# Weight conversion with half the VectorE operations, its pieces listed among the first two groups' chunks

## The chip, the cores and the metric

The kernel runs on one core of a Trainium2 chip. The metric is device microseconds of one execution, as the median of three runs; less is better. The profile is one further execution, recorded by the hardware profiler. PE is TensorE, DVE is VectorE, ACT is ScalarE, POOL is GpSimd and SP is SyncE, whose queue issues nearly all transfers.

## The reference

A gated linear attention (state decayed by a complex gate at every step) feeds a two-layer block with the activation h * cos(h). The two weight matrices arrive as float64, everything else as float32.

```python
mag = sqrt(a_re**2 + a_im**2);  scale = minimum(mag, 0.999) / (mag + 1e-6)
for t in range(768):                                  # B, H, D = 4, 8, 48
    S = (a * scale)[t] * S + outer(k[t], v[t])        # complex gate, real k and v
    y[t] = q[t] @ S.real
x = y.reshape(3072, 384)
h = x @ w_in                                          # w_in [384, 2048], float64
out = (h * cos(h)) @ w_out                            # w_out [2048, 384], float64
```

## The kernel before

The 3072 tokens are 24 chunks of 128 steps; two chunks form a group, so there are 12 groups. The program is a software pipeline over groups. In iteration `it` it emits the gate mathematics of group `it` (`g_log`, `g_prod`, `g_angle`, then `g_phase`, `g_trig`, `g_stack` as `gates`), the attention of group `it - 1` chunk by chunk (`chunks`: transposes `tp`, scores `sc`, state update `sp`, output `yp`, transpose `xp` into `xT`), the first matrix product `mm1` of group `it - 2` (`hp`, then the cosine) and the second, `mm2`, of group `it - 3` (`op`, then the store). `weave` interleaves such lists by a fractional position for each item. A scheduler of the framework then fixes each engine's order; every engine takes its instructions strictly in that order, and so does the SP queue with its transfers.

The gate mathematics of a group is one long chain. ACT takes squares, logarithm and exponentials (L633 to L641), POOL subtracts (`m`, L646), PE forms running sums over the steps (`lgs`, L662), ACT exponentiates them (L663, L664), DVE combines them and closes the angle (`sq`, L688), PE sums the angle (`phs`, L697 and L700), DVE rounds it (`ph`, L702, L704), ACT takes sine and cosine (L712, L713), and DVE builds `ks` and `qs` (L722), which the transposes of the chunk read. DVE masks the scores (`atm`, L746). In `mm1` ACT scales (`turn`, L802), DVE reduces (`cs`, L803, L805), ACT takes the sine, and DVE multiplies by `hp` (`gate`, L807). Lines that go through the helper `special` are recorded as L619, its table loads as L618.

The weights are converted from float64 on the chip. `weight_parts` cuts them into 12 pieces of `w_in` (128 x 512) and 16 of `w_out` (128 x 384); `from_double` loads a piece as 64-bit words into `raw` (two buffers), shifts and joins the words' halves `lo` and `hi` on DVE (L588, L590, L592), takes the rounding bit (L594), adds it on POOL (L596), and clears values too small for float32 (L598, L600). All 28 pieces are woven into iteration 0, beside the gates of group 0:

```python
if it == 0:
    weave((gates(0), 0.0, 1.0), (weights, 0.2, 1.0))
    continue
```

`mm1` of a group needs all of `w_in`, `mm2` all of `w_out`. `gate` has 12 buffers of which a group fills 8; `turn` and `cs` have two each. At the end of the program the flag from `least` decides whether a general path runs; with these inputs it doesn't.

Of the kernel before, what the change touches and what calls it, by code (L numbers as in the profile page):

```python
# [485 lines left out]
def fast_path(ctx, tc, q, k, v, a_re, a_im, moe_w_in, moe_w_out, out, least):  # L486
# [88 lines left out]
    def from_double(dst, src):  # L575

        n = dst.shape[1]
        raw = stage.tile([C, n], I64, tag="raw", name="raw")
        nc.sync.dma_start(out=raw, in_=src)
        words = raw.bitcast(U32).rearrange("p (x two) -> p x two", two=2)
        lo, hi = words[:, :, 0], words[:, :, 1]
        t = stage.tile([C, n], U32, tag="t", name="t")
        bits = dst.bitcast(U32)
        nc.vector.tensor_scalar(out=bits, in0=hi, scalar1=3, scalar2=0x3FFFFFF8,  # L588
                                op0=ALU.logical_shift_left, op1=ALU.bitwise_and)
        nc.vector.scalar_tensor_tensor(out=bits, in0=hi, scalar=0xC0000000, in1=bits,  # L590
                                       op0=ALU.bitwise_and, op1=ALU.bitwise_or)
        nc.vector.scalar_tensor_tensor(out=bits, in0=lo, scalar=29, in1=bits,  # L592
                                       op0=ALU.logical_shift_right, op1=ALU.bitwise_or)
        nc.vector.tensor_scalar(out=t, in0=lo, scalar1=28, scalar2=1,  # L594
                                op0=ALU.logical_shift_right, op1=ALU.bitwise_and)
        nc.gpsimd.tensor_tensor(out=bits, in0=bits, in1=t, op=ALU.add)  # L596
        e = stage.tile([C, n], U32, tag="t", name="t")
        nc.vector.tensor_scalar(out=e, in0=hi, scalar1=20, scalar2=0x7FF,  # L598
                                op0=ALU.logical_shift_right, op1=ALU.bitwise_and)
        nc.vector.scalar_tensor_tensor(out=dst, in0=e, scalar=897.0, in1=dst,  # L600
                                       op0=ALU.is_ge, op1=ALU.mult)
# [135 lines left out]

    def f_scores(n, hh):
# [4 lines left out]
        for h in range(HH):  # L743
            nc.tensor.matmul(ps[:, h], lhsT=y["kT"][:, hh * HH + h], rhs=y["qT"][:, hh * HH + h],  # L744
                             start=True, stop=True)
# [17 lines left out]
    def f_state(n):  # L763
# [4 lines left out]
        for h in range(H):  # L768
            nc.tensor.matmul(ps[:, h], lhsT=X[g]["ks"][:, i * H + h].rearrange("p a d -> p (a d)"),  # L769
                             rhs=X[g]["v"][:, i, h], start=True, stop=True)  # L770
# [20 lines left out]
    def mm1(g, jp):  # L791
# [8 lines left out]
        cs = msb.tile([C, 2, G * C], F32, tag="cs", name="cs")  # L800
        gate = msb.tile([C, 2, G * C], F32, tag="gate", name="gate", bufs=12)
        nc.scalar.activation(out=turn, in_=ps, func=AF.Identity, scale=INV_TWO_PI, bias=quarter_b)  # L802
# [7 lines left out]
    def mm2(g, i):  # L810
# [5 lines left out]
        nc.scalar.copy(out=ot, in_=ps)  # L816
# [33 lines left out]
    weights = weight_parts()  # L850
    for it in range(NG + 3):
# [9 lines left out]
        if it == 0:  # L861
            weave((gates(0), 0.0, 1.0), (weights, 0.2, 1.0))
            continue
        if 0 <= o < NG:
            for i in range(G):
                mm2(o, i)
        weave((gates(g) if g < NG else (), 0.0, 0.5),
              (chunks(c) if 0 <= c < NG else (), 0.0, 1.0),
              ([lambda jp=jp: mm1(m, jp) for jp in range(NJ // 2)] if 0 <= m < NG else (),
# [4 lines left out]
def kernel(ctx, tc, q, k, v, a_re, a_im, moe_w_in, moe_w_out, out):  # L874
# [7 lines left out]
    fast_path(tc, q, k, v, a_re, a_im, moe_w_in, moe_w_out, out, least)  # L882
    low = keep.tile([D2, 1], F32, name="low")
    nc.vector.tensor_reduce(out=low, in_=least, axis=AX.X, op=ALU.min)
    scratch = ctx.enter_context(tc.tile_pool(name="scratch", bufs=1,
                                             space=bass.MemoryType.DRAM))
    line_d = scratch.tile([D2], F32, name="line_d")
    nc.sync.dma_start(out=line_d, in_=low.rearrange("p o -> (p o)"))
    line = keep.tile([1, D2], F32, name="line")
# [39 lines left out]
```

## Time and profile before

| | |
|---|---|
| median of three runs | 931.01 us (930.38 to 933.06) |
| the profiled execution | 938.23 us, its span 936.4 us |
| mean granted TensorE clock | 0.943 |
| PE busy | 797.1 us (85%) |
| DVE busy | 497.1 us (53%) |
| ACT busy | 378.6 us (40%) |
| POOL busy | 171.3 us (18%) |

Busy shares are means over the whole span, and the start differs from the rest. How to read the rows below: the slices are fortieths of the span, with a digit for tenths of busy time; the stage table gives busy time per engine in chosen stretches; a timeline row begins with its start and its length, and ends, in brackets, with the engine's idle time before it and what ended that.

### The profile page before, as it was taken

The page shows a single profiled execution, that of the slowest core. Times are in us where ns is not written, and L with a number is a line of the kernel's source. Part 1 is how long each engine was busy: PE and PEld are TensorE (multiplying, and loading weights), DVE is VectorE, ACT ScalarE, POOL GpSimd, SP SyncE. Part 2 cuts the span into 40 slices and gives each one's busy share as a digit, 9 for nine tenths or more (in the row PEclk, how much of TensorE's full clock was granted, in tenths as well). Part 3 has the DMA queues.
Part 4 walks back from the last instruction along what each step waited for, and adds up shares of the span by engine and source line. Part 5 has one row for each costly group of instructions (what it writes and reads, how often), then busy time and mean ns, then how long its engine had stood idle before and what let it go on. Part 6 is the DMA issues. An engine that isn't in the chain of part 4 may idle for free.

```text
span 936.4 us, 10169 instructions
## 1 busy us (share of the span) xinstructions
PE 797.1 (85%) x3920; PEld 621.0 (66%) x3920; DVE 497.1 (53%) x761; ACT 378.6 (40%) x588; POOL 171.3 (18%) x96
## 2 busy tenths in 40 slices
PE   1101446899999999999999999999999989999997
PEld 0000245685885977967968858858769668778684
DVE  3999985844544736636545446346456445123160
ACT  5222123535454554454364454354544623123140
POOL 2343333403103022112120031031030211000000
PEclk9999966899899999989899999898999998998999
DMA  8523631303004004004023040040040100000000
GB/s 174 141 90 112 146 108 34 69 18 63 23 18 85 1 18 85 1 17 85 1 43 60 18 83 3 18 85 1 18 84 1 26 10 1 9 9 1 9 8 21
DMA packets 151876, 42.03 MB, mean 45 GB/s; under 512 B 144638, under 2 KB 148222, under 8 KB 151818
## 3 DMA queue, kind: packets, MB, share of 16 engines
q1 hardware_dynamic: 151218, 40.98, 19.8%
q8 instruction: 33, 0.54, 0.3%
q10 hardware_dynamic: 600, 0.30, 0.1%
q14 instruction: 25, 0.20, 0.1%
HBM read 36.51 MB, written 4.76 MB: 44 GB/s over the span
## 4 chain that ended last, share of the span: by engine, by line
PE 70%; ACT 6%; DVE 2%; POOL 2%; DMA 1%; issue 1%; ACTq 0%; SPq 0%; POOLq 0%; DVEq 0%
PE hp L796 28%; PE op L813 17%; PE yp L755 4%; PE sc L744 4%; PE yp L758 4%; PE tp L734 4%; PE sp L769 3%; POOL m L646 2%; ACT rs L619 2%; PE lgs L662 1%; ACT L618 1%; PE phs L697 1%; PE phs L700 1%; PE xp L788 1%; ACT m L619 1%; ACT mag L619 1%
## 5 line engine op out<-in xcount | busy, mean ns | idle before, releaser
L796 PE MATMUL hp<-xT,w_in 128*128 128x256 f32 x1152 | 294.0, 409 | 4.1 <-DVE gate L807 3.5
L796 PEld LDWEIGHTS hp<-xT,w_in 128*128 128x128 f32 x1152 | 231.0, 207 | 39.7 <-DVE gate L807 3.9
L813 PE MATMUL op<-w_out,gate 128*128 128x384 f32 x768 | 251.1, 486 | 0.0
L813 PEld LDWEIGHTS op<-w_out,gate 128*128 128x128 f32 x768 | 145.9, 190 | 99.2
L803 DVE TENSOR_SCALAR cs<-turn 128x512 f32<-128x512 f32 x96 | 42.4, 443 | 172.9 <-ACT turn L802 172.9
L802 ACT ACTIVATE turn<-hp,quarter_b 128x512 f32<-128x512 f32 x96 | 65.7, 685 | 124.6 <-PE hp L796 122.7
L807 DVE TENSOR_TENSOR gate<-hp,cs 128x512 f32<-128x512 f32 x96 | 66.2, 690 | 82.2 <-ACT cs L619 81.4
L776 POOL TENSOR_TENSOR state<-state,end 96x384 f32<-96x384 f32 x16 | 31.2, 1949 | 342.2 <-DVE state L774 179.1
L755 PE MATMUL yp<-v,atm 128*128 128x48 f32 x384 | 75.3, 292 | 19.3 <-DVE atm L746 19.3
L619 ACT ACTIVATE cs<-cs 128x512 f32<-128x512 f32 x96 | 60.5, 630 | 69.0 <-DVE cs L805 69.0
L662 PE MATMUL lgs<-m,sums 128*128 128x384 f32 x48 | 21.3, 572 | 64.6 <-POOL m L646 49.3
L755 PEld LDWEIGHTS yp<-v,atm 128*128 128x128 f32 x384 | 62.0, 209 | 20.4 <-DVE atm L746 20.2
L758 PE MATMUL yp<-state,qT 96*128 96x48 f32 x320 | 67.7, 296 | 0.0
L805 DVE TENSOR_TENSOR cs<-turn,cs 128x512 f32<-128x512 f32 x96 | 65.9, 687 | 2.1
L662 PEld LDWEIGHTS lgs<-m,sums 128*128 128x128 f32 x48 | 9.2, 211 | 75.2 <-POOL m L646 71.3
L646 POOL TENSOR_TENSOR m<-m,rs 128x768 f32<-128x768 f32 x12 | 22.0, 1835 | 197.6 <-ACT rs L619 196.7
L697 PE MATMUL phs<-sq,sums 128*128 128x384 f32 x48 | 22.4, 557 | 38.8 <-DVE sq L688 38.8
L758 PEld LDWEIGHTS yp<-state,qT 96*128 96x128 f32 x320 | 54.2, 212 | 0.0
L761 ACT COPY x<-yp 128x384 f32<-128x384 f32 x24 | 11.5, 478 | 104.6 <-PE yp L758 94.0
L633 ACT ACTIVATE m<-re 128x768 f32<-128x768 f32 x12 | 10.1, 842 | 97.3 <-DMA re<-in_a_re_dram 97.3
L744 PE MATMUL sc<-qT,kT 96*128 96x128 f32 x384 | 48.4, 277 | 0.1
L744 PEld LDWEIGHTS sc<-qT,kT 96*128 96x128 f32 x384 | 46.9, 192 | 2.3 <-ACT qT L736 1.0
(77 smaller groups left out, 955.0 us busy)
## 6 DMA issues: line engine op xcount, KB each, us to landing
raw<-in_moe_w_in_dram SPq DMA_DIRECT2D x12, 512.0 KB
raw<-in_moe_w_out_dram SPq DMA_DIRECT2D x16, 384.0 KB
re<-in_a_re_dram SPq DMA_DIRECT2D x24, 192.0 KB
im<-in_a_im_dram SPq DMA_DIRECT2D x24, 192.0 KB
k<-in_k_dram SPq DMA_DIRECT2D x24, 192.0 KB
q<-in_q_dram SPq DMA_DIRECT2D x24, 192.0 KB
v<-in_v_dram SPq DMA_DIRECT2D x24, 192.0 KB
out_dram<-ot SPq DMA_DIRECT2D x24, 192.0 KB
```

Of the source, the lines that this page charges most:

```text
L619: chain(nc.scalar.activation(func=func, **kw))
L646: nc.gpsimd.tensor_tensor(out=m2, in0=m2, in1=rs, op=ALU.subtract)
L662: nc.tensor.matmul(ps, lhsT=sums, rhs=x["lg"][:, ts(i, DM)], start=True, stop=True)
L744: nc.tensor.matmul(ps[:, h], lhsT=y["kT"][:, hh * HH + h], rhs=y["qT"][:, hh * HH + h], start=True, stop=True)
L755: nc.tensor.matmul(ps[:, h], lhsT=y["atm"][:, h], rhs=vals[:, h], start=True, stop=(state is None))
L758: nc.tensor.matmul(ps[:, h], lhsT=y["qT"][:, h], rhs=state[:, h], start=False, stop=True)
L796: nc.tensor.matmul(ps[:, ji], lhsT=w_in[:, dc, ts(jp * 2 + ji, C)], rhs=x["xT"][:, dc].rearrange("p g t -> p (g t)"), start=(dc == 0), sto ...
L802: nc.scalar.activation(out=turn, in_=ps, func=AF.Identity, scale=INV_TWO_PI, bias=quarter_b)
L803: nc.vector.tensor_scalar(out=cs, in0=turn, scalar1=ROUND, scalar2=ROUND, op0=ALU.add, op1=ALU.subtract)
L805: nc.vector.tensor_tensor(out=cs, in0=turn, in1=cs, op=ALU.subtract)
L807: nc.vector.tensor_tensor(out=gate, in0=ps, in1=cs, op=ALU.mult)
L813: nc.tensor.matmul(ps, lhsT=X[g]["gate"][j // 2][:, j % 2, ts(i, C)], rhs=w_out[:, j], start=(j == 0), stop=(j == NJ - 1))
```

## The change

Of a piece's six DVE operations three are left. DVE moves the high word into place (L592 and L594 of the new kernel), and takes the exponent (L598) into `e`, which has one buffer. ACT turns the low word into the missing bits in one operation (`low`, L596), which POOL adds (L597), and sums over each row how far exponents fall below the limit (L600); the sums go to `odd`, which is reduced once and joins the flag at the end, instead of a clearing of each value. The converted weights are twice the true ones, and the scales of `turn` and of the copy out of `mm2` undo that.

The list of pieces is cut in two: `w_in` is woven into iteration 1, among group 0's chunks, `w_out` into iteration 2, among group 1's chunks and the first `mm1`. Iteration 0 is now woven like the others. The reduced angle of `mm1` is written into the gate's own buffer, and the tile `cs` is gone.

```diff
-        t = stage.tile([C, n], U32, tag="t", name="t")
+        low = stage.tile([C, n], U32, tag="low", name="low")
+        e = stage.tile([C, n], U32, tag="e", name="e", bufs=1)
...
-        nc.vector.scalar_tensor_tensor(out=bits, in0=lo, scalar=29, in1=bits,
-                                       op0=ALU.logical_shift_right, op1=ALU.bitwise_or)
-        nc.vector.tensor_scalar(out=t, in0=lo, scalar1=28, scalar2=1,
-                                op0=ALU.logical_shift_right, op1=ALU.bitwise_and)
-        nc.gpsimd.tensor_tensor(out=bits, in0=bits, in1=t, op=ALU.add)
-        e = stage.tile([C, n], U32, tag="t", name="t")
-        nc.vector.tensor_scalar(out=e, in0=hi, scalar1=20, scalar2=0x7FF,
-                                op0=ALU.logical_shift_right, op1=ALU.bitwise_and)
-        nc.vector.scalar_tensor_tensor(out=dst, in0=e, scalar=897.0, in1=dst,
-                                       op0=ALU.is_ge, op1=ALU.mult)
+        nc.scalar.activation(out=low, in_=lo, func=AF.Identity, scale=2.0 ** -29, bias=carrier_b)
+        nc.gpsimd.tensor_tensor(out=bits, in0=bits, in1=low, op=ALU.add)
+        nc.vector.tensor_scalar(out=e, in0=hi, scalar1=1, scalar2=21,
+                                op0=ALU.logical_shift_left, op1=ALU.logical_shift_right)
+        nc.scalar.activation(out=e.bitcast(F32), in_=e, func=AF.Relu, scale=-1.0, bias=least_e_b,
+                             accum_out=odd[:, ds(next(odds), 1)])
...
-        cs = msb.tile([C, 2, G * C], F32, tag="cs", name="cs")
         gate = msb.tile([C, 2, G * C], F32, tag="gate", name="gate", bufs=12)
-        nc.scalar.activation(out=turn, in_=ps, func=AF.Identity, scale=INV_TWO_PI, bias=quarter_b)
+        cs = gate
+        nc.scalar.activation(out=turn, in_=ps, func=AF.Identity, scale=INV_TWO_PI / in_scale,
+                             bias=quarter_b)
...
-        nc.scalar.copy(out=ot, in_=ps)
+        nc.scalar.mul(out=ot, in_=ps, mul=1.0 / (in_scale * out_scale))
...
-    weights = weight_parts()
+    parts = weight_parts()
+    weights = {1: parts[:-NJ], 2: parts[-NJ:]}
...
-        if it == 0:
-            weave((gates(0), 0.0, 1.0), (weights, 0.2, 1.0))
-            continue
...
               (chunks(c) if 0 <= c < NG else (), 0.0, 1.0),
+              (weights.get(it, ()), 0.0, 1.0),
```

DVE's order at group 0's phase, before: behind the last rounding of the phase (`ph`) conversions stand between each pair of the group's own operations, here up to `ks`.

```order
L704 TENSOR_TENSOR ph<-phs,ph 128x384
L588 TENSOR_SCALAR w_in<-raw 128x512
L600 SCALAR_TENSOR_TENSOR w_in<-t,w_in 128x512
...
L710 TENSOR_SCALAR trig<-ph 128x768
...
L635 TENSOR_TENSOR m_515<-m_515,sq 128x768
...
L722 TENSOR_TENSOR ks<-Q,trig 128x1536
```

The same place on DVE in the new kernel:

```order
L711 TENSOR_TENSOR ph<-phs,ph 128x384
L642 TENSOR_TENSOR m_213<-m_213,sq 128x768
L717 TENSOR_SCALAR trig<-ph 128x768
L729 TENSOR_TENSOR ks<-Q,trig 128x1536
L729 TENSOR_TENSOR qs<-P,trig 128x1536
L592 TENSOR_SCALAR w_in<-raw 128x512
```

The conversions have moved from between `ph`, `trig` and `ks` to behind `qs`.

DVE's order in iteration 2, between the phase of group 2 and its `trig`, before:

```order
L702 TENSOR_SCALAR ph<-phs 128x384
L746 TENSOR_TENSOR atm<-sc,causal 128x512
L704 TENSOR_TENSOR ph<-phs,ph 128x384
...
L710 TENSOR_SCALAR trig<-ph 128x768
L774 SCALAR_TENSOR_TENSOR state<-sp,state 96x384
```

The same place in the new kernel, where `w_out` is converted:

```order
L709 TENSOR_SCALAR ph<-phs 128x384
L756 TENSOR_TENSOR atm<-sc,causal 128x512
L711 TENSOR_TENSOR ph<-phs,ph 128x384
L818 TENSOR_TENSOR gate<-hp,gate 128x512
L592 TENSOR_SCALAR w_out<-raw 128x384
L598 TENSOR_SCALAR e<-raw 128x384
L594 SCALAR_TENSOR_TENSOR w_out<-raw,w_out 128x384
L717 TENSOR_SCALAR trig<-ph 128x768
```

Pieces of `w_out` now stand between the operations of group 2, where there was none.

SP's queue around the second half of the weights, before (`end` is the small transfer that closes a group's `g_prod`; `im`, `k`, `re` and `q` are a group's inputs):

```order
L541 DMA q<-in_q_dram 128x8x48 x2
L583 DMA raw<-in_moe_w_out_dram 128x384 x9
L541 DMA v<-in_v_dram 128x8x48 x2
L541 DMA im<-in_a_im_dram 128x8x48 x2
L541 DMA k<-in_k_dram 128x8x48
L675 DMA end<-row 48x16x1 x2
```

The same in the new kernel:

```order
L542 DMA im<-in_a_im_dram 128x8x48 x2
L586 DMA raw<-in_moe_w_out_dram 128x384
L542 DMA k<-in_k_dram 128x8x48
L682 DMA end<-row 48x16x1 x2
L542 DMA re<-in_a_re_dram 128x8x48 x2
L586 DMA raw<-in_moe_w_out_dram 128x384 x2
L542 DMA k<-in_k_dram 128x8x48
L542 DMA q<-in_q_dram 128x8x48 x2
L586 DMA raw<-in_moe_w_out_dram 128x384 x9
```

All pieces of `w_out` from the fourth on now stand behind `end` of group 2.

## Rows read from the trace of the kernel before

**Rows 1.** Page, busy tenths in 40 equal slices of the span

```profile
PE   1101446899999999999999999999999989999997
PEclk9999966899899999989899999898999998998999
```

**Rows 2.** Busy time by stage; columns PE, PEld, DVE, ACT, POOL, clock, DMA, GB/s

```profile
28.35:73.49 45.14, 4.58 (x6) 1.68 (x7) 41.84 (x65) 10.39 (x12) 19.16 (x11) 1.00 0.44 122
73.49:105.86 32.37, 3.78 (x8) 1.96 (x8) 31.21 (x49) 5.55 (x9) 13.03 (x9) 1.00 0.46 110
105.86:156.01 50.15, 28.22 (x155) 24.23 (x155) 38.70 (x88) 11.25 (x18) 17.32 (x13) 0.71 0.36 103
156.01:173.43 17.42, 13.87 (x48) 10.65 (x49) 10.65 (x13) 11.95 (x18) 6.80 (x4) 0.79 0.16 31
173.43:209.15 35.72, 35.72 (x227) 31.61 (x227) 21.89 (x34) 15.56 (x26) 5.96 (x3) 0.89 0.25 45
209.15:232.54 23.39, 22.19 (x69) 12.78 (x68) 11.17 (x12) 12.60 (x17) 8.37 (x4) 1.00 0.25 47
232.54:936.40 703.86, 685.85 (x3407) 536.94 (x3405) 327.89 (x484) 297.87 (x473) 92.32 (x45) 0.96 0.14 29
```

**Rows 3.** Waits before 160 us: who waited for whom, total, times, longest

```profile
PE phs L697 <- DVE sq L688: 38.8, 2, 28.6
PE lgs L662 <- POOL m L646: 38.6, 1, 38.6
PE yp L755 <- DVE atm L746: 19.3, 3, 11.3
```

**Rows 4.** Timeline, one w_in piece and POOL's add: start, length, instruction

```profile
51.99 0.42 DVE L594 TENSOR_SCALAR t<-raw 128x512 uint32<-128x512 uint32 x1
52.32 0.69 DVE L592 SCALAR_TENSOR_TENSOR w_in<-raw,w_in 128x512 uint32<-128x512 uint32 x1
...
53.09 1.37 POOL L596 TENSOR_TENSOR w_in<-w_in,t 128x512 uint32<-128x512 uint32 x1 [2.35 <-DVE w_in L592]
53.26 1.49 DVE L588 TENSOR_SCALAR w_in<-raw 128x512 uint32<-128x512 uint32 x1
```

**Rows 5.** Timeline, one w_out piece, POOL's add, and a product that reads PSUM

```profile
128.06 0.55 DVE L592 SCALAR_TENSOR_TENSOR w_out<-raw,w_out 128x384 uint32<-128x384 uint32 x1
128.53 0.35 DVE L598 TENSOR_SCALAR t<-raw 128x384 uint32<-128x384 uint32 x1
128.69 1.04 POOL L596 TENSOR_TENSOR w_out<-w_out,t 128x384 uint32<-128x384 uint32 x1 [1.88 <-DVE w_out L592]
128.80 0.68 DVE L746 TENSOR_TENSOR atm<-sc,causal 128x512 f32<-128x512 f32 x1
```

**Rows 6.** Groups by line and form: count, busy us, mean ns, idle before

```profile
L807 DVE TENSOR_TENSOR gate<-hp,cs 128x512 f32<-128x512 f32 x96 | 66.2, 690 | 82.2 <-ACT cs L619 81.4
...
L619 ACT ACTIVATE cs<-cs 128x512 f32<-128x512 f32 x96 | 60.5, 630 | 69.0 <-DVE cs L805 69.0
...
L619 ACT ACTIVATE P<-lgs 128x384 f32<-128x384 f32 x24 | 11.8, 492 | 24.3 <-PE lgs L662 24.3
```

**Rows 7.** Timeline, the gate chain of group 0 and of group 3

```profile
9.21 0.93 ACT L619 ACTIVATE m<-m,tiny_b 128x768 f32<-128x768 f32 x1 [1.03 <-DVE m L635]
...
28.35 2.93 PE L697 MATMUL phs<-sq,sums 128*128 128x384 f32 x4 [10.18 <-DVE sq L688]
...
43.97 0.94 ACT L619 ACTIVATE trig<-trig,half_pi_b 128x768 f32<-128x768 f32 x1 [4.33 <-DVE trig L710]
...
213.32 0.94 ACT L619 ACTIVATE m<-m,tiny_b 128x768 f32<-128x768 f32 x1
...
226.23 2.45 DVE L688 SCALAR_TENSOR_TENSOR sq<-sq,rs 128x768 f32<-128x768 f32 x1
```

**Rows 8.** Timeline of SyncE's queue: a row merges issues of one kind

```profile
38.32 37.29 SPq L583 DMA_DIRECT2D raw<-in_moe_w_in_dram  x8
...
111.46 29.23 SPq L583 DMA_DIRECT2D raw<-in_moe_w_out_dram  x9
```

## What is predicted, and how

> **What bounds the kernel now.** I read the page's slices first. In [rows 1] TensorE (PE) stands at 1, 1, 0, 1, 4, 4, 6 tenths in its first seven slices of 23.4 us and at 8 or 9 from the eighth on: the span is a start of about 165 us in which PE mostly waits, and a long stretch in which it is full. The second view, busy time by stage [rows 2], cuts the start at the points where PE gets something new: first phase matmul of group 0 (28.35), first running log sum of group 1 (73.49), first phase matmul of group 1 (105.86), first mm1 (156.01), phase of group 2 (173.43), first mm2 (209.15), the transposes behind that mm2 (232.54). Up to 105.86 VectorE is busy for 41.84 of 45.14 and 31.21 of 32.37 us, and PE for 8.4 us in both together. From 173.43 on PE is busy for 35.72 of 35.72, and for 685.85 of the last 703.86 us. The third view, waits before 160 us [rows 3], names who ends PE's long idle times: POOL's `m`, VectorE's `sq` and `atm`, all of which stand in queues between weight conversions. So the path runs through VectorE until about 150 us and through PE afterwards. Behind 232.54 the order on PE is the same row for row in both kernels, so what can change is the time at which that point is reached, unless the full stretch itself runs at another speed.
>
> **What the change does, by cost.** A w_in piece now has three VectorE shifts at 0.42 us and three two-input operations at 0.68 to 0.69 [rows 4]: 3.3 us. It keeps two of the first and one of the second: 1.52. A w_out piece goes from 3 x 0.35 + 3 x 0.55 = 2.7 to 1.25 us [rows 5]. Over 12 and 16 pieces VectorE loses 21.4 + 23.2 = 44.6 us of work. POOL's add stays, 1.37 and 1.04 us, and it isn't free to VectorE: the shift issued at 53.26, while that add ran, took 1.49 instead of 0.42 [rows 4]. But the `atm` product, which reads PSUM, took its usual 0.68 beside an add of 1.04 [rows 5]. I therefore count POOL's adds as VectorE time except beside PSUM readers. The Trainium skill (SBUF — State Buffer, Who interferes with whom) says the same of the shared port, that the blocked engine waits for the other's whole instruction; both rows agree.
>
> ScalarE gains two operations a piece. The trace has no such form; the nearest rows are 0.63 us at 512 columns and 0.49 at 384 [rows 6], so 12 x 1.26 + 16 x 0.98 = 31 us, and up to twice that if the strided read or the accumulated sum costs extra. In the start ScalarE is busy for 10.39, 5.55, 11.25, 11.95, 15.56 and 12.60 us in 204 [rows 2]; I take the 31 as covered there. The Trainium skill speaks against this move (ScalarE: Activation LUTs, Rules for kernel authors): it wants additions and Relu on VectorE. With the fixed cost and the rate that the same skill page gives for ScalarE, the 56 operations would be an estimated 36 us, which the idle time would cover too.
>
> The other half is the move. The pieces leave the first iteration: two w_in pieces still stand ahead of the first phase (VectorE's order is filled early), the other ten come among group 0's chunks, and all of w_out comes among group 1's chunks and the first mm1. Stage by stage, what the new start should be:
>
> (1) First phase matmul: two more conversion operations and one add ahead of it, 28.35 becomes about 31.
>
> (2) Phase of group 0 to phase of group 1. From 28.35 to the end of the second sine at 43.97 + 0.94 [rows 7] there are 16.6 us, with about three pieces' VectorE work between; without them about 8.2, then the table load: the logarithm of group 1 starts near 40. From there, group 0 needed 28.35 - 9.21 = 19.1 us to its phase matmul, and group 3, with no conversions about, 226.23 + 2.45 - 213.32 = 15.4 [rows 7]. Three w_in pieces lie in this chain now, 3 x (1.52 + 1.37) = 8.7, about two thirds of it in the way. 40 + 19 + 6 = 65, against 105.86. Ends: 55 (nothing in the way) and 70 (all of it and another POOL turn).
>
> (3) To the first mm1: it took 50.15 us with twelve w_out pieces in VectorE's queue [rows 2]. PE's own work is 28.22 us at a granted clock of 0.71; VectorE's is now four w_in pieces (11.6) and the group's own operations. I take 29, so 94 against 156.01. Ends: 22 (the same PE work at full clock and two waits) and 40.
>
> (4) To the phase of group 2: 17.42 before, a chain of the same kind as in (2); the last w_in and first w_out pieces join it, mostly while PE finishes the chunk. 19, so 113. Ends 15 and 27.
>
> (5) From there to the last w_out piece. VectorE's 21.89 and POOL's 5.96 us [rows 2] get 14 pieces x (1.25 + 1.04) = 32 more: 59.9 if nothing overlaps; eight gate products at 0.69 [rows 6] and the four score products at 0.68 [rows 5], with the phase roundings some 11 us, read PSUM, of which I let half lie beside POOL: 54, so 167. Ends: 35.72, where PE alone sets the pace, and 60. PE was full here, so this stage becomes longer, not shorter: VectorE takes the bound back for one iteration.
>
> (6) From the last piece mm2 still has one matmul of its first and sixteen of its second chunk to do, half of the 23.39 us [rows 2] and the wait for the log sums and phase of group 3, which are now closer behind: 15, so 182 against 232.54.
>
> That is 50 us. PE's order lists each conversion's followers strictly, and ScalarE's in-order queue has operations that wait for a piece's transfer; I take 5 off for such waits: **45 us**. Transfers themselves: with two buffers, eight w_in pieces were issued in 37.29 us and nine w_out in 29.23 [rows 8], 4.66 and 3.25 us a piece, paced by VectorE then; 14 x 3.25 = 45.5 would fit under the 54 of (5).
>
> The remaining edits I cost at nothing: the cosine written into the gate's buffer uses one of 12 buffers, of which mm2 has released eight before mm1 needs the ninth; the scaled copy out of mm2 is the same ScalarE operation 24 times, off the path but for the last; the flag's extra reductions and row come before mm2 of group 0. If the gate's cover failed it would be PE waiting in every iteration, and the stretch behind 232.54 would show it.
>
> **Rivals.** (A) POOL and VectorE overlap better than counted, or PE reaches mm2's order first, so stage (5) is PE's 36 to 37 us: mm2 starts near 113 + 36, the join is at 149 + 23.4 = 172, a gain of 60: 871. For it: PE was full there before. Against: 32 us of added VectorE and POOL work where 8 us were free.
>
> (B) Transfers and ScalarE's in-order queue set the pace: SyncE's queue puts the w_out pieces from the fourth on behind `end` of group 2 and the loads of group 3, and each later piece needs its buffer back. With 4.66 instead of 3.25 us a piece [rows 8], 14 x 4.66 = 65 us in stage (5) and a like excess of 4 to 5 us in stage (3): the gain falls to about 30, 901. For it: the addition of waits on an engine that also copies kT and qT. Against: it never showed in the start of before, where VectorE was later than the transfers.
>
> (C) Slower. The same mechanism at full price: the steps above hold about 53 us for conversions (6, 11, 5 and 26 in stages (2) to (5), and the 5 of waits), so a start with none on its path joins at 187 - 53 = 134. If 26 pieces (all but the first two) each held ScalarE's queue for a whole unhidden 4.66 us, that is 121 us on top: the join falls at 255, 22 us late, 953. It decides from (232.54 - 134) / 26 = 3.8 us unhidden per piece. Two buffers, with the next piece's transfer in flight, speak against it.
>
> (D) The gain is given back: the full stretch runs at a granted clock of 0.96 [rows 2], between lower and full level; 45 of 686 us come back if the mean falls to 0.90. PE's order there is unchanged, and the clock fell only around the long waits in 105.86 to 209.15 (0.71, 0.79, 0.89), so nothing points to it. About 931.
>
> **How the numbers follow.** The profiled execution took 938.23 us with a span of 936.4; the median of the three runs is 931.01. The 45 us come from the profiled span, which becomes 891; on the median 931.0 - 45 = **886 us**. Chances: forecast 0.55, A 0.18, B 0.20, C 0.04, D 0.03. For the range I put the ends of (2) to (5) together as independent: shorter by 10, 7, 4 and 18 gives 22 us more gain, longer by 5, 11, 8 and 6 gives 16 less. That is 864 to 902; I take 866 to 904, so that B lies in it and A does. A measurement of this kernel can tell about 0.3% from no change (2.8 us); all but C and D is faster by far more: faster 0.94, same 0.03, slower 0.03.
>
> **What would show it.** In the profile after: no slice under 3 tenths for PE beyond the third; first phase matmul of group 1 near 65, first mm1 near 94, first mm2 between 149 and 169, the transposes behind it near 187; VectorE at 9 tenths until about 165 with POOL's adds between, and PE below full in stage (5). Of the stretch behind the join, 703 us long as before to within 5. Rival A would show PE full from 113; B waits of ScalarE or VectorE on `raw`; C the same with each piece apart; D a lower clock behind the join. I am wrong if the start's chain isn't VectorE's: if stage (2) keeps over 60 us without VectorE being busy, something that this trace hides under it (loads, POOL) sets it.

## The result, and the profile after

| | before | after |
|---|---|---|
| median of four runs each, on one chip | 932.03 us (930.38 to 935.01) | 870.79 us (868.33 to 878.84) |
| the profiled execution, its span | 938.23, 936.4 us | 878.84, 877.0 us |
| mean granted TensorE clock | 0.943 | 0.952 |

The ratio is 0.9355 with a 95% interval of 0.9285 to 0.9424: 61 us faster, where 45 were forecast. The profiled span is 59.4 us shorter. From here on medians and spreads are of all executions of a kernel, and ratios leave out those over 1.5% above its fastest.

The slices of the changed kernel, which answer to [rows 1], with VectorE's beside them:

```profile
PE   1229889899999999999999999999999989999997
...
DVE  3888889664464464464473464464473464034060
...
PEclk9998789989999999999998989999999978989999
```

PE is at 8 or 9 tenths from the fourth slice on, at 66 us, and not from the eighth. VectorE is at 8 or 9 tenths from the second to the seventh.

The stage table of the changed kernel (PE, PEld, DVE, ACT, POOL with their counts, clock, DMA, GB/s), cut at the points of [rows 2], but for the first log sum of group 1: phase of group 0, phase of group 1, first mm1, phase of group 2, first mm2, the transposes behind it:

```profile
30.50:63.94 33.44, 8.31 (x15) 3.65 (x15) 27.25 (x31) 21.53 (x33) 14.19 (x8) 1.00 0.51 129
63.94:91.43 27.49, 25.08 (x155) 21.27 (x155) 23.67 (x35) 20.34 (x37) 9.13 (x7) 0.85 0.51 122
91.43:106.58 15.15, 12.46 (x44) 9.59 (x45) 12.24 (x17) 12.34 (x22) 8.98 (x5) 0.82 0.50 140
106.58:144.91 38.33, 36.05 (x212) 31.41 (x212) 34.84 (x60) 25.59 (x52) 18.98 (x14) 0.87 0.51 125
144.91:171.31 26.40, 24.92 (x88) 14.59 (x87) 19.52 (x34) 20.65 (x36) 10.56 (x9) 1.00 0.37 97
171.31:877.00 705.69, 684.30 (x3407) 535.78 (x3405) 330.62 (x486) 297.45 (x473) 96.58 (x47) 0.96 0.15 29
```

The last boundary, the **join**, has moved from 232.54 to 171.31, by 61.2 us. Behind it PE runs the same 3407 matmuls in 705.69 us, before in 703.86. So the whole gain lies ahead of the join, the point at which PE starts the transposes behind the first mm2. From 63.94 to 171.31 PE is busy for 98.5 of 107.4 us (the four rows added).

The waits of PE in the first 172 us (who waited for whom, total, times, longest), for [rows 3]:

```profile
PE lgs L669 <- POOL m L653: 27.9, 3, 15.6
PE phs L704 <- DVE sq L695: 27.8, 3, 13.2
...
PE op L824 <- POOL w_out L597: 1.2, 2, 0.6
```

`lgs` and `phs` still wait, but nearly all of that lies ahead of 64 us. For the additions that finish converted weights PE waits 1.2 us in all.

### The profile page after: what moved, and what is told of

Its sections match the earlier page's. It is cut to its first block, busy times and chain, and to the rows that moved or that the text cites. A ratio compares the mean times of both kernels' runs of the same rounds, so it can differ in the third digit from the quotient of the medians.

```text
span 877.0 us, 10145 instructions
## 1 busy us (share of the span) xinstructions
PE 794.0 (91%) x3920; PEld 617.5 (70%) x3920; DVE 463.7 (53%) x682; ACT 413.4 (47%) x672; POOL 168.5 (19%) x96
## 4 chain that ended last, share of the span: by engine, by line
PE 68%; ACT 6%; DVE 2%; POOL 2%; DMA 2%; issue 0%; SPq 0%; ACTq 0%; POOLq 0%; DVEq 0%
PE hp L806 28%; PE op L824 17%; PE yp L765 4%; PE sc L754 4%; PE yp L768 4%; PE tp L741 4%; PE sp L780 2%; POOL m L653 2%; ACT rs L626 2%; PE lgs L669 1%; ACT L625 1%; PE phs L704 1%; PE phs L707 1%; PE xp L798 1%; ACT m L626 1%; DMA line_d<-low 1%
## 5 line engine op out<-in xcount | busy, mean ns | idle before, releaser
L806 PE MATMUL hp<-xT,w_in 128*128 128x256 f32 x1152 | 290.3, 405 | 0.9 <-ACT xT L799 0.9
L806 PEld LDWEIGHTS hp<-xT,w_in 128*128 128x128 f32 x1152 | 228.4, 205 | 34.8 <-ACT xT L799 1.3
L814 DVE TENSOR_SCALAR gate<-turn 128x512 f32<-128x512 f32 x96 | 42.8, 447 | 160.0 <-ACT turn L812 159.7
L818 DVE TENSOR_TENSOR gate<-hp,gate 128x512 f32<-128x512 f32 x96 | 66.2, 689 | 75.4 <-ACT gate L626 73.8
L786 POOL TENSOR_TENSOR state<-state,end 96x384 f32<-96x384 f32 x16 | 29.5, 1845 | 322.5 <-DVE state L784 161.9
L626 ACT ACTIVATE gate<-gate 128x512 f32<-128x512 f32 x96 | 60.6, 631 | 61.7 <-DVE gate L816 61.7
L765 PE MATMUL yp<-v,atm 128*128 128x48 f32 x384 | 72.6, 284 | 0.0
L816 DVE TENSOR_TENSOR gate<-turn,gate 128x512 f32<-128x512 f32 x96 | 68.5, 714 | 1.9
L765 PEld LDWEIGHTS yp<-v,atm 128*128 128x128 f32 x384 | 59.7, 201 | 0.8 <-DVE atm L756 0.2
L754 PE MATMUL sc<-qT,kT 96*128 96x128 f32 x384 | 50.3, 282 | 1.0 <-ACT qT L743 1.0
```

Source lines behind the costliest of these rows:

```text
L626: chain(nc.scalar.activation(func=func, **kw))
L765: nc.tensor.matmul(ps[:, h], lhsT=y["atm"][:, h], rhs=vals[:, h], start=True, stop=(state is None))
L806: nc.tensor.matmul(ps[:, ji], lhsT=w_in[:, dc, ts(jp * 2 + ji, C)], rhs=x["xT"][:, dc].rearrange("p g t -> p (g t)"), start=(dc == 0), sto ...
L814: nc.vector.tensor_scalar(out=cs, in0=turn, scalar1=ROUND, scalar2=ROUND, op0=ALU.add, op1=ALU.subtract)
L816: nc.vector.tensor_tensor(out=cs, in0=turn, in1=cs, op=ALU.subtract)
L818: nc.vector.tensor_tensor(out=gate, in0=ps, in1=cs, op=ALU.mult)
```

## The experiments

Two measures are used below. One is the time of the join. The other is for executions that ran at different granted clocks: I multiply the length of a stretch by its granted clock, and call the product full-clock us. It is the time that the stretch would take at the upper level, 2.4 GHz, if PE were busy throughout; where PE waits, it says little, and PE's idle time is given beside it.

How far may two executions of one kernel differ? The changed kernel was run once more, beside three others:

> The changed kernel once more, beside the next three on one chip. Theory: join (transposes behind the first mm2) again at 171 +- 3 us, the stretch behind it 698 to 708 us, median 868 to 873 us. If the median is over 4 us away from 870.8, differences of a few us between the other runs are not to be read at all.

Its join came at 170.10, its median was 873.04 us (861.44 to 877.45, six runs; ratio 0.9292, 0.9241 to 0.9343), its profiled span 872.2. The join of these two executions agrees to 1.2 us, and the phase of group 2 to 1.7 (106.58 and 104.88). The stretch behind the join was 702.1, and 694 to 708 us in all kernels here whose order there is the same, 3407 matmuls. Differences between runs are therefore read at the join first, and differences of 2 us there, or medians within some 4 us of each other, tell nothing.

**The two halves apart.** One kernel only moves the pieces, with the old operations; the other has the new operations and the old place.

```diff
-    weights = weight_parts()
+    parts = weight_parts()
+    weights = {1: parts[:-NJ], 2: parts[-NJ:]}
...
-        if it == 0:
-            weave((gates(0), 0.0, 1.0), (weights, 0.2, 1.0))
-            continue
...
+              (weights.get(it, ()), 0.0, 1.0),
```

That is the first, against the kernel before:

> The old conversion (six VectorE operations a piece), with its pieces listed among the first two groups' chunks as in the changed kernel. Theory (both halves are needed, since VectorE and POOL carry the start): sixteen w_out pieces cost 16 x 1.2 to 1.45 = 19 to 23 us more in the stage before mm2, ten w_in pieces another 8 to 13 us before that; the point behind the first mm2, at 171.3 us in the changed kernel, falls near 200, the time is near 901 to 907. Rival 'the move alone does it': within 8 us of the changed kernel, 871 to 879. Rival 'the halving alone does it': no gain, near 930.

The second is the changed kernel with this diff undone:

> The new conversion, with all 28 pieces woven into the first iteration as before. Theory: VectorE loses 38 to 45 us of work from a start that it bounds until the first mm1, so the gain is 35 to 45 of the 61 us: the point behind the first mm2 falls between 188 and 198, the time is 887 to 897. Rival 'the move alone does it': under 15 us of gain, above 917. Rival 'the halving alone does it': all 61, near 871.

The move alone gave 909.28 us (ratio 0.9722, 0.9654 to 0.9789), the operations alone 899.11 (0.9643, 0.9557 to 0.9729), before 934.52 on that chip. The gains are 25 and 35 us, together 60, as much as the whole change: each part gives about as much alone as with the other in place. Both runs came out some 2 us slower than expected (901 to 907 and 887 to 897). Stage rows of the move alone, from the phase of group 1 to the first mm1, and from the phase of group 2 to the join:

```profile
58.64:99.61 40.97, 31.30 (x154) 26.91 (x154) 29.85 (x49) 14.72 (x21) 13.05 (x9) 0.70 0.41 100
...
123.42:180.68 57.26, 43.33 (x211) 36.05 (x212) 46.63 (x102) 14.96 (x25) 20.57 (x15) 0.80 0.38 98
180.68:207.99 27.31, 26.55 (x89) 15.47 (x90) 18.35 (x36) 11.04 (x18) 9.21 (x7) 0.94 0.22 64
```

And of the operations alone, group 0's phase to group 1's, and the last two stages:

```profile
30.58:82.69 52.11, 8.22 (x14) 3.66 (x14) 48.52 (x58) 33.27 (x59) 28.55 (x17) 0.53 0.57 156
...
139.82:176.82 37.00, 37.00 (x231) 32.64 (x231) 21.59 (x36) 16.86 (x28) 3.58 (x2) 0.89 0.23 40
176.82:200.14 23.32, 22.20 (x69) 12.78 (x68) 11.17 (x12) 12.59 (x17) 8.37 (x4) 1.00 0.26 47
```

Moved at full cost, the pieces let group 1's phase come at 58.64, 47 us earlier than before (and 5.3 earlier than in the changed kernel, with three pieces added by POOL ahead of it instead of four), but the join only 24.5 us earlier: 57.26 us pass to the first mm2, in which PE is busy for 43.33, so PE waits there. Halved but left in place, they keep VectorE busy for 48.52 of 52.11 us ahead of group 1's phase, and PE is idle there. The halving is what makes the pieces small enough to lie beside PE in their new place (in the last two stages PE is idle for 14.7 us with the old operations, for 3.8 in the changed kernel); the move is what empties the first stretch.

**Who sets the time from the first mm1 on: PE or VectorE with POOL?** One kernel takes POOL's additions away (the weights then lack their low bits and the doubling), which leaves the order on PE and on VectorE as it was:

```diff
-        nc.gpsimd.tensor_tensor(out=bits, in0=bits, in1=low, op=ALU.add)
```

> The changed kernel without POOL's add (the weights lack their low bits; everything else runs). PE's order is the same row for row. Theory 'VectorE with POOL sets the stage before mm2' (my forecast): 16 x 1.0 to 1.4 us leave it, the last w_out piece is ready 12 us or more earlier and the point behind the first mm2 moves from 171.3 to 160 or below. Rival 'PE sets it' (PE was busy for 61.0 of 64.7 us from 106.6 on): the pieces are ready earlier, but that point moves by no more than PE's waits there, 4 us, and what the first two stages give, up to 4 more: 163 to 168.

The other adds VectorE work, one more join of 0.55 us for each w_out piece:

```diff
-        nc.vector.scalar_tensor_tensor(out=bits, in0=hi, scalar=0xC0000000, in1=bits,
-                                       op0=ALU.bitwise_and, op1=ALU.bitwise_or)
+        for _ in range(2 if n == DM else 1):
+            nc.vector.scalar_tensor_tensor(out=bits, in0=hi, scalar=0xC0000000, in1=bits,
+                                           op0=ALU.bitwise_and, op1=ALU.bitwise_or)
```

> The changed kernel with the joining operation of each w_out piece issued twice (same result): 16 x 0.55 = 8.8 us more VectorE work between the first mm1 and the first mm2. Theory 'VectorE with POOL sets the stage': the point behind the first mm2 moves from 171.3 to 178 to 181. Rival 'PE sets it': to 175 at most.

Stage rows of the kernel without additions, from the phase of group 2 to the join:

```profile
98.69:135.56 36.87, 32.72 (x211) 29.45 (x212) 28.86 (x64) 24.71 (x52) 7.25 (x3) 0.95 0.57 139
135.56:161.14 25.58, 24.49 (x89) 14.68 (x87) 16.27 (x29) 20.50 (x36) 4.96 (x4) 1.00 0.35 87
```

POOL drops from 29.5 to 12.2 us in these two stages and VectorE from 54.4 to 45.1, and the stages together only from 64.7 to 62.5. PE's idle time in them doesn't fall: it is 5.2 us, with the additions 3.8. At full clock they are 60.6 us (36.87 x 0.95 + 25.58), with the additions 59.7 (38.33 x 0.87 + 26.40). So they are PE's. The conversions aren't quite free there: the kernel before, which had none in these stages, took 55.2 full-clock us (35.72 x 0.89 + 23.39 [rows 2]), with PE idle for 1.2.

Ahead of that point the same kernel is 7.9 us earlier. 4.5 of this lie ahead of group 1's phase (59.49 against 63.94), where PE is mostly idle and VectorE and POOL set the pace. The rest lies in stages that PE nearly fills, at a clock of 0.92 instead of 0.85 up to the first mm1, and can't be put down to the additions alone.

The kernel with 8.8 us of joins added is best compared with the second run of the changed kernel, whose granted clocks ahead of group 2's phase were the same up to the first mm1. Stage from the first mm1 to that phase, and PE's wait for `sq` at its end, first in the second run of the changed kernel, then with the joins:

```profile
89.45:104.88 15.43, 12.63 (x44) 9.68 (x45) 12.30 (x17) 12.20 (x22) 9.16 (x5) 0.81 0.50 141
...
89.45:108.83 19.38, 12.62 (x44) 9.67 (x45) 16.75 (x17) 12.70 (x21) 11.32 (x7) 0.76 0.51 132
```

```profile
PE phs L704 <- DVE sq L695: 2.8, 1, 2.8
...
PE phs L705 <- DVE sq L696: 6.8, 1, 6.8
```

The join came 5.6 us later (175.68 against 170.10), and 4.0 of them are this wait. VectorE was busy for 4.45 us more in the stage, but only 0.55 of that is an added join. The rest are `mag`, a join and `sq`, which took 1.75, 2.15 and 2.55 us instead of 0.94, 0.54 and 0.95: operations of POOL had come to run beside them. So group 2's phase still waits for VectorE's queue and for what POOL does beside it. Behind the phase the other fifteen joins, 8.3 us of work, put the join off by another 1.6 us only, within the scatter. Both joins, 161.14 and 175.68, lie between the ranges of the two expectations, so neither decides by itself; the stages do. The times, one execution each, were 858.36 and 876.76 us.

**ScalarE.** Its operations in the changed kernel, by line and form (count, busy us, mean ns, idle before), up to the join:

```profile
L596 ACT ACTIVATE low<-raw,carrier_b 128x384 uint32<-128x384 uint32 x16 | 10.4, 647 | 1.0 <-POOL w_out L597 0.8 <-DMA raw<-in_moe_w_out_dram 0.2
...
L600 ACT ACTIVATE e<-e,least_e_b 128x384 f32<-128x384 uint32 x16 | 9.8, 613 | 3.8 <-DVE e L598 3.7
L596 ACT ACTIVATE low<-raw,carrier_b 128x512 uint32<-128x512 uint32 x12 | 9.1, 761 | 2.4 <-DMA raw<-in_moe_w_in_dram 2.4
L600 ACT ACTIVATE e<-e,least_e_b 128x512 f32<-128x512 uint32 x12 | 8.6, 720 | 16.9 <-DVE e L598 15.0 <-DVE P L676 1.9
...
L600 ACT ACTIVATION_READ_ACCUMULATOR e<-e,least_e_b 128x1 f32 x28 | 5.3, 190 | 0.0
```

That is 10.4 + 9.8 + 9.1 + 8.6 + 5.3 = 43.2 us, not 31. One kernel does `low` twice, another leaves out L600, and with it the test whether a weight is too small for float32:

```diff
-        nc.scalar.activation(out=low, in_=lo, func=AF.Identity, scale=2.0 ** -29, bias=carrier_b)
+        for _ in range(2):
+            nc.scalar.activation(out=low, in_=lo, func=AF.Identity, scale=2.0 ** -29,
+                                 bias=carrier_b)
```

> The changed kernel with ScalarE's `low` operation issued twice for each piece (same result): 12 x 0.76 + 16 x 0.65 = 19.5 us more ScalarE work. Theory 'ScalarE has room' (forecast): the point behind the first mm2 moves from 171.3 by less than 4 us. Rival 'its in-order queue is on the path' (B): by 8 to 19 us.

```diff
-        nc.scalar.activation(out=e.bitcast(F32), in_=e, func=AF.Relu, scale=-1.0, bias=least_e_b,
-                             accum_out=odd[:, ds(next(odds), 1)])
```

> The changed kernel without ScalarE's second operation of each piece (Relu with its accumulated sum, 28 of them, about 24 us with the read-out instruction): left out is the test whether a weight is too small for float32. Theory 1 (ScalarE's added work is on the path in part, as the run with 19.5 us more of it cost 13 us): join 6 to 14 us earlier, stage (3) and (4) shorter, about 858 to 865 us. Theory 2 (only work beyond what the change adds hits the path, because TensorE or VectorE sets the pace at the present load): join less than 4 us earlier, 867 to 871 us.

Twice `low`: 882.46 us in one execution, the join at 184.39, 13.1 later for 19.5 us of work, so more of it is not free, and the forecast of under 4 us failed. Without L600: 872.08 us (868.32 to 875.70), the join at 171.81, no earlier at all for 23.7 us of work less. The stage table without L600, from the phase of group 1 to the join:

```profile
67.50:93.91 26.41, 24.17 (x155) 20.93 (x155) 20.06 (x33) 17.97 (x27) 8.23 (x6) 0.76 0.47 118
93.91:109.41 15.50, 12.91 (x45) 9.55 (x45) 11.02 (x13) 8.76 (x14) 9.49 (x6) 0.80 0.44 119
109.41:145.89 36.48, 34.57 (x211) 30.30 (x212) 35.30 (x66) 19.21 (x33) 15.38 (x13) 0.91 0.59 144
145.89:171.81 25.92, 24.92 (x88) 14.52 (x87) 20.58 (x30) 17.68 (x26) 13.76 (x10) 1.00 0.36 94
```

ScalarE is down from 78.9 to 63.6 us in these stages, their length from 107.4 to 104.3; ahead of them the phase of group 1 came 3.6 us later. Both edits also let the scheduler set many of VectorE's and ScalarE's rows in another order, so a difference of a few us can't be put down to ScalarE alone. What holds is this: at the present size ScalarE's work is covered but for some 3 us, and more of it isn't. With `low` twice, these rows of ScalarE stood in group 2's chain:

```profile
99.82 0.77 ACT L597 ACTIVATE low<-raw,carrier_b 128x512 uint32<-128x512 uint32 x1 [3.24 <-DMA raw<-in_moe_w_in_dram]
100.50 0.92 ACT L628 ACTIVATE rs<-rs,one_b 128x768 f32<-128x768 f32 x1
101.32 0.75 ACT L597 ACTIVATE low<-raw,carrier_b 128x512 uint32<-128x512 uint32 x1
```

`rs`, a logarithm in group 2's chain, waited behind a `low` that waited 3.24 us for its transfer; the stage from the first mm1 to group 2's phase took 25.76 us instead of 15.15. The wait is a part of these 10.6 us; ScalarE also had 30 rows in the stage instead of 22, and what each cost wasn't taken apart. The other long stage, to the first mm1, took 36.78 us at a clock of 0.64 instead of 27.49 at 0.85: at full clock 23.5 and 23.4, but with PE idle for 6.6 us instead of 2.4, so both the clock and waits made it longer.

**Transfers.** One `raw` buffer instead of two:

```diff
-        raw = stage.tile([C, n], I64, tag="raw", name="raw")
+        raw = stage.tile([C, n], I64, tag="raw", name="raw", bufs=1)
```

> The changed kernel with one buffer for the raw words in place of two, so that no piece's transfer runs while the one before is converted. Theory 'two buffers hide the transfers, and a bare one costs 3.3 to 4.7 us a piece' (mechanism of my slower rival C): 26 pieces x about 3 us unhidden, less what the gate chain covers: the point behind the first mm2 moves from 171.3 to 210 to 240. Rival 'transfers have ample room': to 185 at most.

It ran in 880.96 us, one execution, 10 above the changed kernel's median and 2 above its slowest, far less than a wait for every transfer would make. The scheduler had spread the pieces out: the last w_out addition came at 218.87, 61 us later than in the changed kernel, and PE's order had other work in between. So this run doesn't measure what a wait for a transfer costs at the old places, which stays open. It has the transfers' own time (issues by line; KB of each, median us from issue to landing):

```profile
raw<-in_moe_w_in_dram SPq DMA_DIRECT2D x12, 512.0 KB, 3.7
raw<-in_moe_w_out_dram SPq DMA_DIRECT2D x16, 384.0 KB, 3.1
```

**The cosine in the gate's buffer**, changed alone in the kernel before:

```diff
-        cs = msb.tile([C, 2, G * C], F32, tag="cs", name="cs")
+        cs = gate
```

> The kernel before with the cosine's angle written into the gate's buffer, the one edit of the change that touches the full stretch. My forecast: nothing; the stretch from the point behind the first mm2 (232.5) to the end stays 704 us within 8, and the time within that of the kernel before. If the gate's buffer came free too late, PE would wait in each of eleven iterations, 1 us or more each.

931.74 us in one execution against a median of 932.68 on the same chip, the join at 230.9, 699.0 us behind it: nothing.

**Another order of the lists.** If PE sets the time from 64 us on, is there more to be had by giving it work earlier? One kernel lists seven steps of group 0's first chunk ahead of group 1's gates, one weaves w_out later into iteration 2, one does both:

```diff
+        early = ()
+        if it == 1:
+            early = list(chunks(0))
+            for t in early[:7]:
+                t()
...
-              (chunks(c) if 0 <= c < NG else (), 0.0, 1.0),
+              (early[7:] if early else chunks(c) if 0 <= c < NG else (), 0.0, 1.0),
```

> The changed kernel, with the first seven steps of group 0's chunk list (transposes, scores, state) written ahead of group 1's gate chain in iteration 1. Theory 'PE sets the start from 64 us on, and is idle before': about 10 of PE's 25 us of chunk work move under group 1's chain, first mm1 from 91.4 to 80 to 84, the point behind the first mm2 from 171.3 to 160 to 164, the time near 861. Rival 'VectorE is still the bound before the first mm1' (busy 27.3 of 33.4 us there, POOL 14.2): the chain of group 1 is pushed back by what the chunk adds, and the point moves by less than 4 us.

```diff
-              (weights.get(it, ()), 0.0, 1.0),
+              (weights.get(it, ()), 0.0 if it == 1 else 0.4, 1.0),
```

> The changed kernel with the w_out pieces woven from 0.4 to 1.0 of iteration 2 instead of 0.0 to 1.0. Theory 1 (ScalarE's in-order queue and VectorE delay group 2's gate chain through the pieces that stand in it): stage (4), first mm1 to group 2's phase, shrinks from 15.15 to about 11 to 12 us, the join comes 3 to 5 us earlier, about 866 us. Theory 2 (TensorE alone sets the path from the first mm1 on): join within 2 us of the changed kernel, median within 2 us. Later pieces could also make mm2 wait on POOL's w_out adds: then over 5 us of such waits (1.2 us in the changed kernel) and a join up to 8 us later.

> The same later w_out pieces together with the first seven steps of group 0's chunk listed ahead of group 1's gate chain. Theory 1: group 2's phase, which waited 13.5 us for VectorE's sq when the chunk alone was listed first, comes at 95 to 100 us instead of 104, the join at 157 to 162, median 860 to 865 us. Theory 2 (the gate chain of group 2 is paced by its own operations and by group 1's chain, not by conversions): phase of group 2 still at 102 to 105, join at 164 to 168, median within 3 us of the changed kernel.

The chunk first gave 869.25 us (ratio 0.931, 0.927 to 0.935), w_out later 877.68 (0.9398, 0.936 to 0.9437), both 875.22 (0.9349, 0.930 to 0.9398). None can be told from the changed kernel as faster. With the chunk first, mm1 began at 79.02 instead of 91.43, but the phase of group 2 came at 104.29 instead of 106.58. Its stage row and its one long wait there:

```profile
79.02:104.29 25.27, 11.78 (x44) 9.37 (x45) 23.41 (x26) 18.39 (x33) 15.88 (x10) 0.70 0.49 137
```

```profile
PE phs L704 <- DVE sq L695: 13.5, 1, 13.5
```

VectorE is busy for 23.41 of 25.27 us, 16.0 of them with conversions (five w_in pieces, one of them in part, and the first of w_out), and PE waits 13.5 for group 2's `sq`: PE work done sooner is waited for later. The join came 5 us earlier than in the first run of the changed kernel, 3.8 than in the second, between the two expectations.

With both, mm1 began at 78.53, the phase of group 2 came at 106.12 and the join at 171.64. That doesn't clear the conversions: the same five w_in pieces and the first of w_out still stand ahead of `sq` in VectorE's order, so the later weave took next to nothing out of group 2's chain. With w_out later alone, the phase of group 2 came 1.9 us earlier than in the first run of the changed kernel and 0.2 earlier than in the second, but the join 6.5 and 7.7 us later. Stage rows from that phase to the join, and three slices of 5 us from them:

```profile
104.67:153.72 49.05, 46.17 (x230) 40.87 (x231) 33.44 (x61) 25.72 (x51) 17.55 (x13) 0.72 0.43 105
153.72:177.82 24.10, 23.41 (x69) 12.36 (x68) 17.81 (x30) 20.66 (x38) 11.89 (x9) 1.00 0.31 87
...
115.00:120.00 5.00, 5.00 (x30) 5.00 (x29) 3.09 (x6) 2.31 (x4) 0.00 (x0) 0.50 0.74 198
120.00:125.00 5.00, 5.00 (x26) 5.00 (x25) 4.52 (x4) 0.25 (x1) 2.27 (x1) 0.50 0.00 0
125.00:130.00 5.00, 5.00 (x18) 4.36 (x19) 0.00 (x0) 1.02 (x2) 0.00 (x0) 0.52 0.00 0
```

The same slices of the changed kernel:

```profile
115.00:120.00 5.00, 5.00 (x20) 4.21 (x20) 4.16 (x10) 4.31 (x9) 0.00 (x0) 0.50 1.04 243
120.00:125.00 5.00, 5.00 (x40) 4.82 (x40) 5.00 (x9) 2.29 (x6) 2.43 (x3) 0.92 0.62 171
125.00:130.00 5.00, 5.00 (x37) 4.67 (x36) 4.29 (x6) 2.61 (x5) 2.52 (x2) 1.00 0.01 2
```

At full clock the two stages are 59.4 us (49.05 x 0.72 + 24.10), in the changed kernel 59.7. PE did the same work, but stayed at the lower level, 1.2 GHz, for 15 us on end instead of about 5 (and from 145 to 155 us its granted clock was 0.66, in the changed kernel 1.00). Ahead of the fall PE had waited 2.88 us for `ph`, in the changed kernel 1.71 and 0.57; behind it the scores, state products and `yp` ran in one piece, where the changed kernel has mm1 matmuls between them. Which of these held the clock down wasn't tried.

## Why the prediction was right, and where it was short

The time, 870.79 us, lies in the stated range of 866 to 904, 15 us under the forecast, and what came is rival A, to which the prediction gave 0.18. (Worked out, the range is 864 to 902; A's 871 and B's 901 lie in it without the 2 us by which I moved it.)

**The bound before was read rightly, its end in the kernel after too late.** Ahead of group 1's phase the path ran through VectorE, and the two halves of the change each gave their part. But the forecast let VectorE keep the bound until the last w_out piece, near 167 us; in the trace PE is the one that is nearly full from group 1's phase on, at 64 us, with VectorE's chain close beside it up to group 2's phase; behind that phase PE sets the time nearly alone. Nothing behind the join changed: 705.69 against a forecast of 703 to within 5, so rival D, the gain given back by the clock, didn't come; nor did C.

Stage by stage, forecast against trace:

| stage | forecast | after |
|---|---|---|
| (1) first phase matmul | 31 | 30.50 |
| (2) to the phase of group 1 | 34 | 33.44 |
| (3) to the first mm1 | 29 | 27.49 |
| (4) to the phase of group 2 | 19 | 15.15 |
| (5) to the last w_out piece | 54 | 52.37 |
| (6) to the join | 15 | 12.36 |
| taken off for in-order waits | 5 | at most 2.7, inside (4) |

The stages are 10.7 us shorter than the forecast, whatever waits they hold, and nothing had to be added to them for the 5 of waits: that is the 15.7 us between a join at 187 and one at 171.31.

**(1) to (3) held in length, (1) and (2) by their mechanism.** Counting POOL's additions as VectorE time was right there: without them group 1's phase comes 4.5 us earlier, and group 1's logarithm starts at 40.10, where the forecast had it near 40. In (3) PE is busy for 25.08 of 27.49 us, so its length is PE's more than that of the pieces. How an operation of POOL holds VectorE is seen in two pairs of rows of the changed kernel's timeline (start, length, instruction; first VectorE, then POOL, whose second row is an addition):

```profile
23.05 2.04 DVE L598 TENSOR_SCALAR e<-raw 128x512 uint32<-128x512 uint32 x1
25.02 1.49 DVE L592 TENSOR_SCALAR w_in<-raw 128x512 uint32<-128x512 uint32 x1
...
22.67 2.14 POOL L725 TENSOR_TENSOR Q<-k,Q 128x768 f32<-128x768 f32 x1 [5.32 <-ACT low L596]
24.77 1.45 POOL L597 TENSOR_TENSOR w_in<-w_in,low 128x512 uint32<-128x512 uint32 x1
```

Each shift ends 0.3 us behind POOL's operation (25.09 and 24.81, 26.51 and 26.22) and takes 2.04 and 1.49 us, where one alone takes 0.42 [rows 4]. The Trainium skill (SBUF — State Buffer, Who interferes with whom) says that the blocked engine waits for the other's whole instruction; the trace agrees.

**(4) was mis-sized**, 19 for 15.15, the low end of its range. I charged the pieces to the chain, but PE is busy for 12.46 of the 15.15 us, and without POOL's additions the stage still takes 14.59 (from 84.10 to 98.69 in that kernel): most of the pieces' work lies beside PE. PE and VectorE's chain end close together there. Taking POOL's additions away gained little; in the kernel with the joins doubled, three of VectorE's operations that met POOL's made the phase 4.0 us later.

**(5) and (6): the length was right for the wrong reason.** I wrote "VectorE takes the bound back for one iteration" and let mm2 follow the last piece. In the trace mm2 begins at 144.91, 14.0 us ahead of the last piece's end at 158.95; five additions lie beside it, and PE waits 1.2 us for them. From group 2's phase to the join PE is busy for 61.0 of 64.7 us. This is rival A, PE setting the pace: A had mm2 at 149, the join at 172 and 871 us; the trace has 144.9, 171.3 and 870.8. That A's number fits to 1 us is luck: it started these stages 6.4 us too late (113 for 106.58) and made them 5.3 us too short (59.4 for 64.7). The kernel without additions shows the same: VectorE busy for 45 instead of 54 us, PE no less idle, and the stages within 1 us at full clock. The argument that misled me was a sum: VectorE's and POOL's work in (5), 59.9 us by my count, was laid end to end in one stage, where PE's order lets the last five pieces lie beside mm2.

**The 5 us for waits** on transfers were more than the trace shows, but such waits exist. The changed kernel has one in group 2's chain (timeline rows of ScalarE, POOL, VectorE and PE):

```profile
94.01 0.77 ACT L596 ACTIVATE low<-raw,carrier_b 128x512 uint32<-128x512 uint32 x1 [1.07 <-DMA raw<-in_moe_w_in_dram]
...
95.51 1.27 POOL L597 TENSOR_TENSOR w_in<-w_in,low 128x512 uint32<-128x512 uint32 x1 [1.36 <-DVE w_in L594]
96.73 1.94 POOL L655 TENSOR_TENSOR mag<-mag,sq 128x768 f32<-128x768 f32 x1
...
93.95 0.48 DVE L592 TENSOR_SCALAR w_in<-raw 128x512 uint32<-128x512 uint32 x1 [3.35 <-DMA raw<-in_moe_w_in_dram]
...
106.58 1.08 PE L704 MATMUL phs<-sq,sums 128*128 128x384 f32 x2 [2.70 <-DVE sq L695]
```

VectorE waits 3.35 us and ScalarE 1.07 for the last w_in piece, POOL's addition follows them, group 2's `mag` stands behind the addition, and at the end of that chain PE waits 2.70 us for `sq`. How much of the 2.70 the transfer made wasn't tried.

**"ScalarE covered" was right in the main, with a wrong size.** The added operations took 43.2 us, not 31: 5.3 are the read-outs of the sums, and about 5 more an estimate for the bias tile that both operations read and the rows of the forecast [rows 6] did not (at 768 columns `m` with `tiny_b` took 0.93 us [rows 7], `mag` without one 0.83; 56 x 0.09). Taking 23.7 us of them away moved the join by 0.5. But the cover is less than I took for granted: 19.5 us more cost 13. A `low` that holds ScalarE's order while it waits for its piece is rival B's mechanism; it exists, and behind 64 us the longest wait of PE that it can be part of is the 2.7 us above. The Trainium skill (ScalarE: Activation LUTs, Rules for kernel authors) wants such work on VectorE; here VectorE was the bound, and the operations alone gained 35 us. By the fixed cost and the rate on the same page of the Trainium skill 36 us were estimated; 37.9 were measured without the read-outs of the sums.

**The small edits** cost nothing that shows, as forecast: the cosine's buffer by its own run, the scaled copy and the flag by the stretch behind the join, which stayed within its scatter of 694 to 708 us.

**What is left.** No run here that does all the work beats the changed kernel by more than medians scatter. Between 64 us and the join PE is idle for only some 9 us; its granted clock was 0.85, 0.82 and 0.87 in the stages up to 144.91, which at full clock would be up to 12 us shorter (27.49 x 0.15 + 15.15 x 0.18 + 38.33 x 0.13). Ahead of 64 us lie the gates of two groups, one after the other.

## What to carry to other kernels

When work is moved from an engine that is the bound to the side of one that will be, don't add its pieces up in a stage of their own: ask by which point the consumer needs each piece, and let the rest lie beside the consumer. Moving the pieces and halving them were worth 25 and 35 us apart and 60 together: measure each part alone before you call one of them the cause. And compare stretches that PE fills by length times granted clock: two kernels 8 us apart did the same work at different clocks.

## What the hardware showed unexpectedly

- An activation with an accumulated sum is followed by an instruction of its own that reads the sum out: 28 of them, 0.190 us each, 5.3 us.
- ScalarE reading every second 32-bit word and writing 32-bit integers took 0.761 us at 512 columns and 0.647 at 384, against 0.63 and 0.49 for f32 [rows 6], which read no bias tile; by the estimate of 0.09 us for that tile, some 0.04 to 0.07 us are left for the stride and the integers.
- With one `raw` buffer a piece of 512 KB took 3.7 us from issue to landing, one of 384 KB 3.1, where I had 4.66 and 3.25 from issues paced by VectorE.
- After a wait of 2.88 us PE stayed at half clock for 15 us (0.50, 0.50, 0.52) although it was busy throughout, in the kernel with w_out woven later.
- POOL is held by VectorE as well: the addition that began at 102.86 in the changed kernel, while VectorE's `P`, `Q`, `rs` and `sq` followed one another, took 4.77 us, in its second run 6.11, against 1.04 [rows 5].
